# Groups of half a sequence, a ramp of 7, 9, 17, and one queue for the first loads, in a fused convolution and feed-forward kernel

## The chip, the cores and the metric

One core of one Trainium2 chip. The metric is the device time of one launch in microseconds (us); medians are over repeated launches. PE is the matmul engine (TensorE), PEld its weight load, DVE is VectorE, ACT is ScalarE, POOL is GpSimd; SP issues most transfers here. PSUM is the memory that PE writes its results into; this kernel takes eight buffers of 512 columns from it in a ring (`bufs=8`, tiles of `[P, 512]`), called banks here. "L264" in a profile line is a line of that kernel's source.

## The reference, cut to what matters

x is 8 sequences of 4224 tokens of 192 values. A causal convolution with 7 taps (one set of softmax weights for each of 8 heads), then layer normalisation, a feed-forward of 192 to 768 with relu and back to 192, and a residual sum:

```python
out = np.einsum('hk,bskhg->bshg', w, x_unf)          # 7 taps, 8 heads of 24 values
xn  = (x - mu) / np.sqrt(var + 1e-06) * g_ln
ch  = np.maximum(xn @ w_ch1, 0.0) @ w_ch2            # 192 -> 768 -> 192
return (x + ch).astype(np.float32)
```

w_ch1 and w_ch2 arrive as 64-bit floats and are rebuilt as 32-bit on the chip.

## The kernel before: the parts that matter

A partition holds 33 consecutive tokens ("runs") of a sequence. A group is some of these runs, for all 128 partitions. The small groups of the first sequence are called the ramp, since with them the pipeline fills; a seam is the change from one PE piece (an up or a down projection) to the next, and the tail is what follows the last matmul. For each group, VectorE convolves, transposes and takes statistics; PE does the up projection (tile `ph`), ScalarE the relu, PE the down projection (`po`), VectorE the scaled residual sum, which also empties `po`.

```python
J = 11
for b in range(B):
    sizes = [J] * (R // J) + [R % J] * (R % J > 0)   # 11, 11, 11
    if b == 0:
        rest = R - 15
        sizes = [7, 8, rest // 2, rest - rest // 2]  # 7, 8, 9, 9
...
nc.gpsimd.dma_start(out=ga, in_=g_col[0:P, :])       # gains: q0 software_dynamic in the profile
nc.sync.dma_start(out=taps, ...)
nc.scalar.dma_start(out=raw1[:, 1:3] ...)            # w1 on two queues, beside x
...
def up(g):                                           # 6 f-blocks
    for f in range(NF):
        ph = [psum.tile([P, 512], F32, tag="ps", ...) for q in range(NQ)]   # 4 of 8 banks
        for c in range(NC):
            for q in range(NQ):
                nc.tensor.matmul(ph[q][:, 0 : n * C], w1[rows, c, fs], t[rows, 0:n, c, :], ...)
        for q in range(NQ):
            nc.scalar.activation(ht[g][:, f, 0:n, q, :], ph[q]..., AF.Relu)

def down(g):
    for i0 in range(0, n, 2):                        # one bank for two runs
        po = psum.tile([P, 512], F32, tag="ps", ...)
        ...                                          # 6 matmuls a run
        nc.vector.scalar_tensor_tensor(out=yg[:, j, :], in0=dst, ...)       # empties it

first_tap(0); conv(0); centre_w1(); first_tap(1); transpose(0)
...                                                  # rebuild w2
for g in range(NG):
    if g + 2 < NG: load_x(g + 2)
    if g == 0: conv(1)
    up(g)
    if g + 1 < NG:
        if g > 0: first_tap(g + 1); conv(g + 1)
        transpose(g + 1)
    stats(g)
    down(g)
```

On VectorE the order within one pass of the loop is thus: convolve and transpose the next group, statistics of this group, then empty this group's `po`.

## Time and profile before

| | before |
|---|---|
| time, first three launches | 1081.26, 1082.58, 1081.49 us |
| span of the profiled execution | 1080.5 us |
| PE / DVE / ACT busy | 98% / 76% / 22% |

The profiled execution took 1082.24 us, so it is a little slower than the median launch. The engine table and the chain that ended last are in the prediction, with their lines.

### The profile page before, as it was taken

The numbers are of one execution on the slowest core, as the hardware profiler recorded it, in microseconds if no ns is written. First come the engines' busy times: TensorE is split into PE (matmuls) and PEld (weight loads), VectorE is DVE, ScalarE is ACT, GpSimd is POOL, SyncE is SP. The second block draws the span as 40 slices with busy tenths as digits, with TensorE's granted clock in tenths as the row PEclk, the third lists the DMA queues.
The fourth block names the chain that finished last, engine by engine and source line by source line (L and its number), as shares of the span: only waits on it lengthen the run. The fifth ranks groups of instructions, "written<-read, shape, count | busy, mean of one in ns | idle before, by whom it ended". The sixth has DMA issues, their size and how long they took to land.

```text
span 1080.5 us, 24335 instructions
## 1 busy us (share of the span) xinstructions
PE 1057.4 (98%) x10512; PEld 898.8 (83%) x10512; DVE 822.2 (76%) x2363; ACT 240.3 (22%) x636; POOL 16.9 (2%) x23
## 2 busy tenths in 40 slices
PE   3999999999999999999999999999999999999998
PEld 3999987978978879789788797897887978978878
DVE  5999798696696876966968769669687696696821
ACT  3521122031131220311312203113122031131220
POOL 3000000000000000000000000000000000000000
PEclk9999999999999999999999999999999999999999
DMA  8022022022022020230220302203202022020011
GB/s 241 2 82 89 4 96 96 30 75 103 2 103 89 16 104 31 74 103 1 104 102 3 103 31 74 104 1 103 102 2 103 32 73 104 1 104 41 2 42 41
DMA packets 9195, 70.55 MB, mean 65 GB/s; under 512 B 1280, under 2 KB 2304, under 8 KB 3329
## 3 DMA queue, kind: packets, MB, share of 16 engines
q1 hardware_dynamic: 8768, 68.02, 18.3%
q8 instruction: 82, 1.34, 0.5%
q10 hardware_dynamic: 224, 0.98, 0.4%
q14 instruction: 25, 0.20, 0.1%
q0 software_dynamic: 96, 0.00, 0.0%
HBM read 43.05 MB, written 25.95 MB: 64 GB/s over the span
## 4 chain that ended last, share of the span: by engine, by line
PE 96%; DVE 2%; DMA 1%; issue 0%; ACT 0%; ACTq 0%; DVEq 0%
PE po L352 48%; PE ph L329 48%; DVE y L265 1%; DMA raw<-in_moe_w_ch_dram 1%; DVE yt L273 0%; DVE w1f L184 0%; DVE scale1a L174 0%; ACT scale1b L166 0%; DVE scale1b L174 0%; DVE power1a L163 0%; DVE mant1a L157 0%; DVE power1a L159 0%; DVE y L357 0%; ACTq L130 0%; DVE power1b L163 0%
## 5 line engine op out<-in xcount | busy, mean ns | idle before, releaser
L352 PEld LDWEIGHTS po<-w,ht 128*128 128x128 f32 x3168 | 513.5, 190 | 13.3 <-issue 11.7
L352 PE MATMUL po<-w,ht 128*128 128x192 f32 x3168 | 522.5, 327 | 0.0
L329 PE MATMUL ph<-yt,w 32*128 32x352 f32 (+3 forms) x7200 | 520.4, 444 | 1.0 <-DVE yt L273 1.0
L329 PEld LDWEIGHTS ph<-yt,w 32*128 32x128 f32 x7200 | 367.4, 185 | 146.1 <-issue 5.4
L265 DVE SCALAR_TENSOR_TENSOR y<-xg,taps,y 128x264 f32<-128x264 f32 (+3 forms) x1200 | 473.7, 474 | 0.0
L334 ACT ACTIVATE ht<-ph 128x352 f32<-128x352 f32 (+3 forms) x600 | 222.7, 459 | 792.3 <-PE ph L329 792.3
L357 DVE SCALAR_TENSOR_TENSOR y<-po,r,y 128x192 f32<-128x192 f32 x264 | 96.5, 412 | 228.0 <-PE po L352 225.3
L286 DVE BATCH_NORM_STATS2 st<-y 128x6 f32<-128x192 f32 x264 | 70.1, 341 | 0.0
L273 DVE STREAM_TRANSPOSE yt<-y 128x2112 f32<-128x2112 f32 (+3 forms) x25 | 57.3, 2290 | 0.9
L257 DVE TENSOR_SCALAR y<-xg,taps 128x264 f32<-128x264 f32 (+1 forms) x184 | 51.4, 351 | 0.0
L237 PE MATMUL pw<-w1f,centre 128*128 128x128 f32 x144 | 18.0, 292 | 18.7 <-DVE w1f L184 18.7
L237 PEld LDWEIGHTS pw<-w1f,centre 128*128 128x128 f32 x144 | 17.9, 208 | 18.6 <-issue 18.6
L101 POOL MEMSET xg<- 1x1152 f32 x8 | 8.4, 1048 | 779.6 <-DVE y L265 779.6
L312 DVE SCALAR_TENSOR_TENSOR r<-d,r 128x11 f32<-128x11 f32 (+3 forms) x75 | 12.7, 170 | 2.6
L308 DVE TENSOR_TENSOR d<-r 128x11 f32<-128x11 f32 (+3 forms) x75 | 12.7, 170 | 2.6
L309 DVE SCALAR_TENSOR_TENSOR d<-d,v 128x11 f32<-128x11 f32 (+3 forms) x75 | 12.7, 170 | 2.6
L240 ACT COPY w<-pw 128x512 f32<-128x512 f32 (+1 forms) x12 | 5.7, 477 | 8.8 <-PE pw L237 8.6
L255 ACT ACTIVATE y<-xg,taps 128x168 f32<-128x168 f32 (+1 forms) x16 | 5.6, 432 | 0.0
L157 DVE TENSOR_SCALAR mant1a<-raw 128x768 uint32<-128x768 uint32 x1 | 0.6, 559 | 6.0 <-DMA raw<-in_moe_w_ch_dram 6.0
L289 DVE TENSOR_TENSOR d<-st 128x11 f32<-128x11 f32 (+3 forms) x25 | 4.4, 177 | 0.9
L300 DVE TENSOR_SCALAR d<-v 128x11 uint32<-128x11 uint32 (+3 forms) x25 | 4.3, 173 | 0.9
L297 DVE TENSOR_SCALAR v<-v 128x11 f32<-128x11 f32 (+3 forms) x25 | 4.3, 173 | 0.9
(46 smaller groups left out, 47.4 us busy)
## 6 DMA issues: line engine op xcount, KB each, us to landing
xg<-in_x_dram SPq DMA_DIRECT2D x14, 1632.0 KB, 9.2
out_dram<-y SPq DMA_DIRECT2D x20, 1056.0 KB, 4.9
xg<-in_x_dram SPq DMA_DIRECT2D x7, 1428.0 KB, 10.8
xg<-in_x_dram SPq DMA_DIRECT2D x2, 1440.0 KB, 12.5
out_dram<-y SPq DMA_DIRECT2D x2, 864.0 KB, 4.4
xg<-in_x_dram SPq DMA_DIRECT2D x1, 1344.0 KB, 14.1
xg<-in_x_dram SPq DMA_DIRECT2D x7, 191.2 KB
raw<-in_moe_w_ch_dram SPq DMA_DIRECT2D x1, 1152.0 KB
```

What stands on the lines that cost most here:

```text
L237: nc.tensor.matmul(dst, m[:, c, :], w1f[:, s, o : o + P], start=start, stop=not start)
L257: nc.vector.tensor_scalar(out=dst, in0=src, scalar1=tap, scalar2=None, op0=ALU.mult)
L265: nc.vector.scalar_tensor_tensor(out=y[g][:, 0:n, cs], in0=t[:, k : k + n, cs], scalar=taps[:, h, k : k + 1], in1=y[g][:, 0:n, cs], op0=AL ...
L273: nc.vector.transpose(yt[g][:, 0:n].rearrange("p j c t -> p (j c t)"), y[g][:, 0:n].rearrange("p j d -> p (j d)"),)
L286: nc.vector.bn_stats(out=st[:, j, :], in_=y[g][:, j, :])
L308: nc.vector.tensor_tensor(d, r, r, op=ALU.mult)
L309: nc.vector.scalar_tensor_tensor(out=d, in0=d, scalar=-0.5, in1=v, op0=ALU.mult, op1=ALU.mult)
L312: nc.vector.scalar_tensor_tensor(out=r, in0=d, scalar=1.5, in1=r, op0=ALU.add, op1=ALU.mult)
L329: nc.tensor.matmul(ph[q][:, 0 : n * C], w1[rows, c, fs], t[rows, 0:n, c, :], start=(c == 0), stop=(c == NC - 1),)
L334: nc.scalar.activation(ht[g][:, f, 0:n, q, :], ph[q][:, 0 : n * C].rearrange("p (j t) -> p j t", t=C), AF.Relu,)
L352: nc.tensor.matmul(dst, t[:, f, j, :, :].rearrange("p q t -> p (q t)"), w2[:, f, :], start=(f == 0), stop=(f == NF - 1),)
L357: nc.vector.scalar_tensor_tensor(out=yg[:, j, :], in0=dst, scalar=rstd[g][:, j : j + 1], in1=yg[:, j, :], op0=ALU.mult, op1=ALU.add,)
```

## The change

Its intent: fewer and larger groups, so fewer seams and fewer fixed costs on VectorE, and an earlier start, since w1 no longer shares the DMA engines with x (before, from 6 to 8 us, the queue that brings most of w1 took 60.1% of the 16 engines' time and SP's, with x and the rest of w1, 42.8%). Groups are 16 and 17 runs (the first sequence 7, 9, 17). 17 runs are 544 columns and do not fit the 512 of one bank, so they are halved to 9 and 8. Buffers of the setup are laid into the space of the first hidden tile to make room, and x has two buffers instead of three.

```diff
-    J = 11
+    J = 17
...
-        sizes = [J] * (R // J) + [R % J] * (R % J > 0)
-        if b == 0:
-            rest = R - 15
-            sizes = [7, 8, rest // 2, rest - rest // 2]
         j0 = 0
-        for n in sizes:
+        for n in (7, 9, R - 16) if b == 0 else (J - 1, J):
...
-    xpool = ctx.enter_context(tc.tile_pool(name="xin", bufs=3))
+    xpool = ctx.enter_context(tc.tile_pool(name="xin", bufs=2))
...
-    raw1 = setup.tile([P, 3, FH, 2], U32, name="raw1")
+    room = hpool.tile([P, NF * J * P], F32, tag="ht", name="room")
+    raw1 = carve(6 * FH, U32).rearrange("p (s f w) -> p s f w", f=FH, w=2)
...
-    nc.gpsimd.dma_start(out=ga, in_=g_col[0:P, :])
+    nc.scalar.dma_start(out=ga, in_=g_col[0:P, :])
...
-    nc.scalar.dma_start(
+    nc.sync.dma_start(
         out=raw1[:, 1:3].rearrange("p s f w -> p (s f w)"), in_=w1_words[0:P, :]
...
-        (nc.sync, nc.scalar)[r].dma_start(
+        nc.sync.dma_start(
...
+        half = n if n * C <= 512 else (n + 1) // 2
         for f in range(NF):
-            ph = [psum.tile([P, 512], F32, tag="ps", name=f"ph{g}_{f}_{q}") for q in range(NQ)]
+            for i0 in range(0, n, half):
+                js = slice(i0, min(i0 + half, n))
```

The small operations on the taps also move ahead of the rebuilding of w1, the rebuilding works in place, and the last group's stores end at 4, 8, 12, 14, 16, 17 runs.

More of the change, by code (lines that the diff above doesn't have):

```diff
@@ L56 @@
     FH = F // 2
-    assert D == P + Q and S % P == 0 and J * C <= 512 and NF % 2 == 0
+    assert D == P + Q and S % P == 0 and R % 2 and R // 2 + 1 == J and NF % 2 == 0
     groups = []
     for b in range(B):
-        sizes = [J] * (R // J) + [R % J] * (R % J > 0)
-        if b == 0:
-            rest = R - 15
-            sizes = [7, 8, rest // 2, rest - rest // 2]
         j0 = 0
-        for n in sizes:
+        for n in (7, 9, R - 16) if b == 0 else (J - 1, J):
             groups.append((b, j0, n))
             j0 += n
-        assert j0 == R and max(sizes) <= J
+        assert j0 == R
+    assert max(n for _, _, n in groups) <= J
     NG = len(groups)
@@ L117, with carve @@
     gb = consts.tile([P, 1], F32, name="gb")
-    raw1 = setup.tile([P, 3, FH, 2], U32, name="raw1")
+    room = hpool.tile([P, NF * J * P], F32, tag="ht", name="room")
+    taken = [0]
+    def carve(n, dtype):
+        part = room[:, taken[0] : taken[0] + n].bitcast(dtype)
+        taken[0] += n
+        return part
+    raw1 = carve(6 * FH, U32).rearrange("p (s f w) -> p s f w", f=FH, w=2)
     raw2 = setup.tile([P, NF * D, 2], U32, name="raw2")
@@ L122 @@
     g_col = moe_g_ln.rearrange("(d o) -> d o", o=1)
-    nc.gpsimd.dma_start(out=ga, in_=g_col[0:P, :])
+    nc.scalar.dma_start(out=ga, in_=g_col[0:P, :])
     for r in range(2):
-        nc.gpsimd.dma_start(out=gb[Q * r : Q * r + Q, :], in_=g_col[P:D, :])
+        nc.scalar.dma_start(out=gb[Q * r : Q * r + Q, :], in_=g_col[P:D, :])
     nc.sync.dma_start(
@@ L148, with split_words @@
     nc.vector.memset(low, -896.0 * (1 << 23))
-    def split_words(raw, name):
-        n = raw.shape[1]
+    def split_words(raw, mant, power):
         hi = raw[:, :, 1]
-        mant = setup.tile([P, n], I32, name="mant" + name)
-        power = setup.tile([P, n], I32, name="power" + name)
-        high = setup.tile([P, n], F32, name="high" + name)
-        scale = setup.tile([P, n], I32, name="scale" + name)
         nc.vector.tensor_single_scalar(mant.bitcast(U32), hi, 0xFFFFF, op=ALU.bitwise_and)
-        nc.scalar.activation(high, mant, AF.Relu, scale=2.0**-20, bias=1.0)
+        nc.scalar.activation(mant.bitcast(F32), mant, AF.Relu, scale=2.0**-20, bias=1.0)
         nc.vector.tensor_scalar(
@@ L165, in split_words, with join_words @@
         )
-        nc.scalar.activation(scale, power, AF.Relu, scale=float(1 << 23), bias=low)
-        return high, scale
-    def join_words(dst, raw, high, scale, gain=None):
+        nc.scalar.activation(power, power, AF.Relu, scale=float(1 << 23), bias=low)
+    def join_words(dst, raw, mant, power, gain=None):
         lo, hi = raw[:, :, 0], raw[:, :, 1]
+        mant, power = mant.bitcast(F32), power.bitcast(U32)
         nc.vector.scalar_tensor_tensor(
-            out=high, in0=lo, scalar=2.0**-52, in1=high, op0=ALU.mult, op1=ALU.add
+            out=mant, in0=lo, scalar=2.0**-52, in1=mant, op0=ALU.mult, op1=ALU.add
         )
         nc.vector.scalar_tensor_tensor(
-            out=scale.bitcast(U32), in0=hi, scalar=0x80000000, in1=scale.bitcast(U32),
+            out=power, in0=hi, scalar=0x80000000, in1=power,
             op0=ALU.bitwise_and, op1=ALU.bitwise_or,
         )
+        power = power.bitcast(F32)
         if gain is None:
-            nc.vector.tensor_tensor(dst, high, scale.bitcast(F32), op=ALU.mult)
+            nc.vector.tensor_tensor(dst, mant, power, op=ALU.mult)
             return
@@ L184, in join_words @@
             nc.vector.scalar_tensor_tensor(
-                out=dst[:, part], in0=high[:, part], scalar=g, in1=scale.bitcast(F32)[:, part],
+                out=dst[:, part], in0=mant[:, part], scalar=g, in1=power[:, part],
                 op0=ALU.mult, op1=ALU.mult,
             )
-    w1f = setup.tile([P, 3, FH], F32, name="w1f")
+    w1f = carve(3 * FH, F32).rearrange("p (s f) -> p s f", f=FH)
     raw1a = raw1[:, 0:2].rearrange("p s f w -> p (s f) w")
@@ L199 @@
     nc.scalar.activation(taps, taps, AF.Exp)
-    parts_a = split_words(raw1a, "1a")
     nc.vector.tensor_reduce(wsum, taps, axis=AX.X, op=ALU.add)
@@ L206 @@
     )
-    join_words(w1f[:, 0:2].rearrange("p s f -> p (s f)"), raw1a, *parts_a, (gb, ga))
-    parts_b = split_words(raw1b, "1b")
-    join_words(w1f[:, 2], raw1b, *parts_b, (ga,))
+    words_a = (raw1a, carve(2 * FH, I32), carve(2 * FH, I32))
+    words_b = (raw1b, carve(FH, I32), carve(FH, I32))
+    split_words(*words_a)
+    join_words(w1f[:, 0:2].rearrange("p s f -> p (s f)"), *words_a, (gb, ga))
+    split_words(*words_b)
+    join_words(w1f[:, 2], *words_b, (ga,))
     w1 = consts.tile([P, NC, F], F32, name="w1")
@@ L218 @@
     for i, (p0, p1, base) in enumerate(((0, P, 0), (0, Q, P), (Q, P, P))):
-        m = setup.tile([P, NC, NQ, C], F32, name=f"centre{i}")
+        m = carve(NC * P, F32).rearrange("p (c q i) -> p c q i", c=NC, q=NQ)
         if p1 - p0 < P:
@@ L322, in up @@
         ht[g] = hpool.tile([P, NF, J, NQ, C], F32, tag="ht", name=f"ht{g}")
+        half = n if n * C <= 512 else (n + 1) // 2
         for f in range(NF):
             fs = slice(f * P, f * P + P)
-            ph = [psum.tile([P, 512], F32, tag="ps", name=f"ph{g}_{f}_{q}") for q in range(NQ)]
-            for c in range(NC):
+            for i0 in range(0, n, half):
+                js = slice(i0, min(i0 + half, n))
+                w = (js.stop - js.start) * C
+                ph = [
+                    psum.tile([P, 512], F32, tag="ps", name=f"ph{g}_{f}_{i0}_{q}")
+                    for q in range(NQ)
+                ]
+                for c in range(NC):
+                    for q in range(NQ):
+                        rows = slice(C * q, C * q + C)
+                        nc.tensor.matmul(
+                            ph[q][:, 0:w], w1[rows, c, fs], t[rows, js, c, :],
+                            start=(c == 0), stop=(c == NC - 1),
+                        )
                 for q in range(NQ):
-                    rows = slice(C * q, C * q + C)
-                    nc.tensor.matmul(
-                        ph[q][:, 0 : n * C], w1[rows, c, fs], t[rows, 0:n, c, :],
-                        start=(c == 0), stop=(c == NC - 1),
-                    )
-            for q in range(NQ):
-                nc.scalar.activation(
-                    ht[g][:, f, 0:n, q, :],
-                    ph[q][:, 0 : n * C].rearrange("p (j t) -> p j t", t=C), AF.Relu,
-                )
+                    nc.scalar.activation(
+                        ht[g][:, f, js, q, :],
+                        ph[q][:, 0:w].rearrange("p (j t) -> p j t", t=C), AF.Relu,
+                    )
     def down(g):
@@ L342, in down @@
         yg = y.pop(g)
-        ends = (n,) if g + 1 < NG else (4, 8, 10, n)
+        ends = (n,) if g + 1 < NG else (4, 8, 12, 14, 16, n)
         done = 0
@@ L374 @@
     transpose(0)
-    parts = split_words(raw2, "2")
-    join_words(w2flat, raw2, *parts)
+    words_2 = (
+        raw2, setup.tile([P, NF * D], I32, name="mant"), setup.tile([P, NF * D], I32, name="power")
+    )
+    split_words(*words_2)
+    join_words(w2flat, *words_2)
     for g in range(NG):
```

## The prediction

> **What bounds the kernel now.** I read the page's engine table first, then the chain that ended last, then the groups by shape, then the timeline where groups meet.
>
> ```profile
> PE 1057.4 (98%) x10512; PEld 898.8 (83%) x10512; DVE 822.2 (76%) x2363; ACT 240.3 (22%) x636; POOL 16.9 (2%) x23
> ```
>
> TensorE is busy 98% of the 1080.5 us span, and VectorE has a quarter of its time free. Saving VectorE instructions is worth nothing by itself. The chain says which PE pieces there are and what comes ahead of them (start, length, what):
>
> ```profile
> 1.20 11.83 DMA raw<-in_moe_w_ch_dram
> ...
> 21.27 14.70 DVE y L265 x48
> ...
> 37.71 14.71 PE ph L329 x283
> 52.43 13.85 PE po L352 x84
> 66.27 16.88 PE ph L329 x288
> 83.15 15.80 PE po L352 x96
> 98.95 17.67 PE ph L329 x288
> 116.62 17.75 PE po L352 x108
> ...
> 1033.92 21.51 PE ph L329 x288
> 1055.44 21.71 PE po L352 x132
> ```
>
> The time is thus three terms: 37.7 us before the first up projection (load w1, rebuild it, convolve group 0, transpose), then 1039.4 us in which up (ph) and down (po) pieces follow without a gap, then a tail of 3.3 us. A change can only shorten the prologue, the cost of a seam between pieces, or the tail; and it can open a gap.
>
> The seams: a group of 9 runs costs 17.67 and one of 11 21.51 in ph. The timeline shows relu evictions of successive f-blocks at steps of 2.27, 2.59, 2.91 and 3.55 us for 7, 8, 9 and 11 runs: 0.03 + 0.32 x runs. Six steps leave 0.21 us per up piece. The down piece is 0.20 + 1.95 x runs (evictions of two runs every 3.90 us), plus 0.05 at 11 runs, a wait for ScalarE.
>
> ```profile
> 66.20 16.95 PE L329 MATMUL ph<-yt,w 32*128 32x256 f32 x288
> ...
> 67.52 2.37 DVE L357 SCALAR_TENSOR_TENSOR y<-po,r,y 128x192 f32<-128x192 f32 x7
> 69.15 1.22 ACT L334 ACTIVATE ht<-ph 128x256 f32<-128x256 f32 x4 [15.94 <-PE ph L329]
> 69.61 13.14 PEld L329 LDWEIGHTS ph<-yt,w 32*128 32x128 f32 x236 [0.36 <-DVE y L357]
> ...
> 72.42 1.21 ACT L334 ACTIVATE ht<-ph 128x256 f32<-128x256 f32 x4 [2.05 <-PE ph L329]
> 75.01 1.21 ACT L334 ACTIVATE ht<-ph 128x256 f32<-128x256 f32 x4 [1.38 <-PE ph L329]
> ```
>
> This is the one existing stall after the prologue. The second f-block of group 1 (8 runs) needs the PSUM buffers of group 0's down piece; VectorE, in program order behind convolution, transpose and statistics, empties them only from 67.52 to 69.89. The block was due at 66.20 + 2.59 = 68.8, so 1.1 us are lost: 16.88 against 6 x 2.59 + 0.21 = 15.75. PSUM buffers go round in a ring of 8, and a late VectorE stops PE through it.
>
> [...]306, 331, 356 and 406 ns pitch (busy over count) for 7, 8, 9 and 11 runs is 131 + 25 x runs. [...]768 KB of w1 on ACT's queue took 8.7 us to land beside x.
>
> **The change, part by part.**
>
> *Steady state.* 25 groups become 17, but the halving makes the 17-run groups two blocks, 9 and 8 wide: still 25 blocks and 7200 up matmuls, and 3168 down. One batch before: 3 x (21.51 + 21.70) = 129.63. After: up(16) = 6 x (0.03 + 5.12) + 0.21 = 31.11; up(17) = 6 x (2.91 + 2.59) + 0.21 = 33.21; down(17) = 0.20 + 33.15 = 33.35. For down(16), the first run's sixth matmul pair needs all four relu evictions of the last f-block.
>
> ```profile
> 536.97 1.53 ACT L334 ACTIVATE ht<-ph 128x352 f32<-128x352 f32 x4 [2.02 <-PE ph L329]
> ...
> L352 PE MATMUL po<-w,ht x25: 326/326/430, 536.9 to 540.9; 128*128 128x192 f32 x25
> ```
>
> The four take 1.53 us at 352 columns, and a matmul of that stretch waits up to 0.1 us (430 against 326 ns). At 224 columns they take 1.11, so 0.82 ns a column each; at 512, 2.05. The wait grows by 0.52 to 0.57: down(16) = 0.20 + 31.20 + 0.57 = 31.97. Batch after: 31.11 + 31.97 + 33.21 + 33.35 = 129.64. The seams saved are given back to ScalarE: **0.0 us** in seven batches. VectorE saves 8 x 48 x 131 ns = 50 us, all off the path. In steady state it reaches the evictions about 40 us into a 17-run group (taps 2.8, convolution of 16 runs 25.5, transpose 3.4, statistics 7.7), 6.6 us after down starts: 3.4 runs, two banks, so no stall.
>
> *Prologue.* The windows show what the first loads share:
>
> ```profile
> 6.00:8.00 2.00, 0.00 (x0) 0.00 (x0) 0.43 (x2) 0.25 (x1) 1.89 (x3) 1.00 1.04 198
> ...
> 20.00:22.00 2.00, 2.00 (x12) 2.00 (x11) 1.83 (x5) 2.00 (x8) 0.00 (x0) 1.00 1.01 430
> ```
>
> (last column GB/s). w1 is 1.18 MB and was complete at 13.0. Alone in order it starts when the 128 small packets of taps are through (5.3 in the packet list) and needs 2.7 us at 430 GB/s or 5.4 at 220, then about 1 us to be seen: 9.1 to 11.7. I take 10.3, so 2.9 us earlier. The four small tap operations (14.70 to 15.52) now run before w1 lands; the join still waits for ScalarE, so I count 0.6. x for group 0 follows in the queue at about 11 to 16 and is wanted by ScalarE some 6.3 us after w1, 16.6: hidden. Centring on PE, 18.0 us from 15.2, ends at 33.2, before the transpose. The rest (convolution of 7 runs, 14.7; transpose, 1.6) is as before: up(0) starts at **34.2, gain 3.5 us**.
>
> *Ramp 7, 9, 17.* Counted from the start of up(0). VectorE before: evictions of group 0 from 29.8 to 32.2. Convolving 9 runs instead of 8 adds 48 x 25 ns = 1.2, transpose 0.2: 31.2 to 33.6. up(1) starts at 28.5, and its second block is due at 31.4: stall 33.6 - 31.4 = 2.2. down(1) ends at 28.5 + 17.67 + 2.2 + 17.75 = 66.1. VectorE meanwhile: first tap of 17 runs (8 x 360 ns = 2.9) to 36.4, convolution 48 x (131 + 425) = 26.7 to 63.0, transpose (178 + 200 x 17 = 3.6) to 66.6, statistics of 9 (5.55) to 72.1, first pair of evictions to 72.8. up(2) needs the transpose at 66.6, and then four PSUM buffers. down(1) holds five of eight, so the fourth comes free only at 72.8. PE **stalls 6.7 us**. In the kernel before, the group there had 9 runs and its evictions began at 96.06, ahead of PE at 98.9: no stall. Stalls go from 1.1 to 8.9: +7.8. The first batch has one group less: 0.4 saved. Convolving 16 runs during group 2 catches up, so the stall is paid once.
>
> *Tail.* Last store one run of 96 KB in both: 0.
>
> Sum: 1081.5 - 3.5 + 7.8 - 0.4 + 0.0 = **1085.4 us**.
>
> **The rivals.** (1) The seams are really won: no ScalarE wait at 512 columns, 7 x 0.57 = 4.0 us less, 1081.4. For it: [...]only 0.1 us is seen now. Against: the eviction time per column is a clean line. (2) The ramp stall does not come, if something empties down(1) sooner: 1085.4 - 7.8 = 1077.6. For it: someone chose 9 and 17 on purpose. Against: VectorE keeps program order in every stretch of the timeline, and the 1.1 us stall shows the mechanism. (3) The early w1 is no gain, because the slow stretch from 6 to 17 us has another cause than sharing (it still moves 203 to 257 GB/s after ACT's queue is done): up to 1088; or the full 430 GB/s: 1084. (4) Two x buffers instead of three expose a load. A 17-run load is 23 x 96 KB = 2.2 MB, some 13 us scaled from 9.2 us for 1632 KB, issued about 65 us ahead: hidden. If not, each group could lose microseconds, 1100 and more; I give it little.
>
> **Range and chances.** Terms (1) and (3) can each move the sum by 3 to 4 us, the stall by 1.5: 1081 to 1089 holds it 8 times in 10. 2% is 21.6 us, far outside all but rival (4). Faster 0.01, within 2% 0.98, slower 0.01.
>
> **What would show it.** In the changed profile: first up matmul at about 34; w1 complete near 10; a gap or lengthened ph piece of 6 to 7 us about 66 us after that, with the PE load waiting for the VectorE eviction of group 1; from then up pieces of 31.1 and 33.2 and down pieces of 32.0 and 33.4; a wait of 0.6 us at each 16-run seam; VectorE busy near 770. A first up start above 36, no stall at group 2, or down(16) of 31.4 would each mark its step wrong; waits for x in mid kernel would make the whole prediction wrong.

The marked cuts take out what no trace of this case shows. The sum came to 1081.5 - 3.5 + 7.8 - 0.4 + 0.0 = 1085.4 us. Its 0.03 + 0.32 x runs and 131 + 25 x runs are fits to the steps and pitches read from the trace; what the 0.03 is made of was not shown. The "about 1 us to be seen" is read from the kernel before: from the end of a load's last packet to the moment it counts as landed the trace has 1.1 us for the taps (5.5 to 6.6) and 1.0 and 1.6 for w1's loads on ScalarE's queue.

## The result, and the profile after

The changed kernel takes 1089.37 us (median of 6, 1088.55 to 1089.68), the kernel before 1081.34 (6 launches). The ratio is 1.0072, 95% interval 1.0059 to 1.0085. Ratios here are the mean time of one kernel's fast runs over that of the other's in the same rounds, so not quite the ratio of the medians quoted. The measured time lies just above the stated range.

The engine table of the changed kernel:

```profile
PE 1060.4 (97%) x10512; PEld 905.1 (83%) x10512; DVE 744.6 (68%) x1779; ACT 240.3 (22%) x636; POOL 15.2 (1%) x20
```

As many matmuls as before, 3 us more PE time, 78 us less VectorE time. The chain of the changed kernel (start, length, what):

```profile
2.25 7.71 DMA room<-in_moe_w_ch_dram
...
15.02 19.24 PE pw L241 x144
...
98.42 3.58 DVE yt L277
...
107.52 0.75 DVE y L369 x2
108.32 35.71 PE ph L341 x549
144.03 33.35 PE po L364 x204
177.38 31.15 PE ph L341 x288
208.53 2.05 ACT ht L346 x4
210.62 29.84 PE po L364 x182
240.47 33.21 PE ph L341 x576
```

Before, the chain was PE without a break from 37.7 us on. Now it runs through VectorE up to 108.3 us: that is the ramp in which PE waits. w1 is complete at 10 us instead of 13. From 144 us on it is again PE, with one 2.05 us piece of ScalarE in each 16-run group. And one piece stands out: the same 17-run up projection takes 35.71 us at 108.32 and 33.21 us later. The timeline where it starts:

```profile
83.82 17.82 PE L364 MATMUL po<-w,ht 128*128 128x192 f32 x108
102.15 0.76 PE L341 MATMUL ph<-yt,w 32*128 32x288 f32 x6 [0.51 <-DVE yt L277]
107.52 3.02 DVE L369 SCALAR_TENSOR_TENSOR y<-po,r,y 128x192 f32<-128x192 f32 x9
108.32 21.88 PE L341 MATMUL ph<-yt,w 32*128 32x288 f32 x332 [5.41 <-DVE y L369]
```

The down projection of group 1 ends at 101.6. Six matmuls of group 2 go out when its transpose is done; the next needs a PSUM bank that VectorE starts to empty at 107.52. From 101.6 to 108.3, 6.7 us, PE does next to nothing. What follows is in the window table (stretch and its length, then busy time of PE, PEld, DVE, ACT and POOL with the number of instructions that fall into the stretch, then the granted PE clock, the DMA share and GB/s):

```profile
102.00:106.00 4.00, 0.76 (x6) 0.34 (x6) 3.74 (x19) 0.00 (x0) 0.00 (x0) 1.00 0.00 0
107.00:108.00 1.00, 0.00 (x0) 0.00 (x0) 0.82 (x4) 0.00 (x0) 0.00 (x0) 0.50 0.00 0
108.50:113.00 4.50, 4.50 (x40) 3.35 (x44) 4.50 (x15) 0.00 (x0) 0.00 (x0) 0.50 0.39 141
114.00:119.00 5.00, 5.00 (x92) 4.48 (x88) 5.00 (x11) 2.10 (x7) 0.00 (x0) 1.00 1.01 419
```

While PE waits, its granted clock falls to 0.50 (at 106.48 us in the trace's clock record), and it stays there until 113.30, for the first five microseconds after the wait: 40 matmuls in 4.5 us where 92 fit into 5 us later. "PE busy" reads 4.50 of 4.50 in the slow stretch; only the clock and the count tell.

### The profile page after: what moved, and what is told of

Same layout as the page of the kernel before. It is cut to its first block, busy times and chain, and to the rows that moved or that the text cites. A ratio compares the mean times of both kernels' runs of the same rounds, so it can differ in the third digit from the quotient of the medians.

```text
span 1087.9 us, 23679 instructions
## 1 busy us (share of the span) xinstructions
PE 1060.4 (97%) x10512; PEld 905.1 (83%) x10512; DVE 744.6 (68%) x1779; ACT 240.3 (22%) x636; POOL 15.2 (1%) x20
## 4 chain that ended last, share of the span: by engine, by line
PE 90%; DVE 7%; ACT 2%; DMA 1%; issue 0%; SPq 0%; DVEq 0%
PE ph L341 45%; PE po L364 44%; DVE y L269 4%; PE pw L241 2%; ACT ht L346 1%; DMA room<-in_moe_w_ch_dram 1%; DVE yt L277 1%; DVE st L290 0%; DVE y L369 0%; DVE y L261 0%; DVE mant L172 0%; DVE w L181 0%; DVE power L175 0%; DVE room L186 0%; DVE d L312 0%
## 5 line engine op out<-in xcount | busy, mean ns | idle before, releaser
L341 PE MATMUL ph<-yt,w 32*128 32x288 f32 (+3 forms) x7200 | 522.2, 445 | 7.3 <-DVE y L369 5.7
L269 DVE SCALAR_TENSOR_TENSOR y<-xg,taps,y 128x408 f32<-128x408 f32 (+3 forms) x816 | 423.6, 603 | 0.0
L346 ACT ACTIVATE ht<-ph 128x288 f32<-128x288 f32 (+3 forms) x600 | 222.6, 457 | 790.5 <-PE ph L341 790.5
L277 DVE STREAM_TRANSPOSE yt<-y 128x3264 f32<-128x3264 f32 (+3 forms) x17 | 55.8, 3284 | 0.6
L261 DVE TENSOR_SCALAR y<-xg,taps 128x408 f32<-128x408 f32 (+1 forms) x120 | 41.8, 422 | 0.0
L241 PE MATMUL pw<-room 128*128 128x128 f32 x144 | 19.2, 304 | 15.0 <-DVE room L186 15.0
L241 PEld LDWEIGHTS pw<-room 128*128 128x128 f32 x144 | 19.1, 220 | 15.0 <-issue 15.0
L312 DVE TENSOR_TENSOR d<-r 128x17 f32<-128x17 f32 (+3 forms) x51 | 9.0, 176 | 1.8
L313 DVE SCALAR_TENSOR_TENSOR d<-d,v 128x17 f32<-128x17 f32 (+3 forms) x51 | 9.0, 176 | 1.8
L316 DVE SCALAR_TENSOR_TENSOR r<-d,r 128x17 f32<-128x17 f32 (+3 forms) x51 | 8.9, 175 | 1.8
```

The lines of the kernel that those rows point to most:

```text
L241: nc.tensor.matmul(dst, m[:, c, :], w1f[:, s, o : o + P], start=start, stop=not start)
L261: nc.vector.tensor_scalar(out=dst, in0=src, scalar1=tap, scalar2=None, op0=ALU.mult)
L269: nc.vector.scalar_tensor_tensor(out=y[g][:, 0:n, cs], in0=t[:, k : k + n, cs], scalar=taps[:, h, k : k + 1], in1=y[g][:, 0:n, cs], op0=AL ...
L277: nc.vector.transpose(yt[g][:, 0:n].rearrange("p j c t -> p (j c t)"), y[g][:, 0:n].rearrange("p j d -> p (j d)"),)
L312: nc.vector.tensor_tensor(d, r, r, op=ALU.mult)
L313: nc.vector.scalar_tensor_tensor(out=d, in0=d, scalar=-0.5, in1=v, op0=ALU.mult, op1=ALU.mult)
```

## The experiments

My theory after reading this: the ramp costs what the prediction said, the 6.7 us wait, and **the wait also costs the clock**. The rivals: the large groups themselves cost in the steady state; the single queue costs; the slow matmuls after the wait have another reason than the clock. Each kernel ran five rounds beside the kernel before on the same chip, so ratios, not medians, are what compares across sections.

### ramp_7_8_8_10: the ramp alone

```diff
-        for n in (7, 9, R - 16) if b == 0 else (J - 1, J):
+        for n in (7, 8, 8, 10) if b == 0 else (J - 1, J):
```

> The changed kernel with the first sequence as 7, 8, 8, 10 in place of 7, 9, 17; all else as changed. Theory (a late VectorE holds the PSUM buffers of group 1, PE idles 6.7 us before group 2 and then runs at half clock): the stall and the half clock after it go, PE pieces of the first sequence end near 167.5 us instead of 177.4, so about 1079.5 us, 10 us under the changed kernel. Rival one, the cost is in the large groups of the steady state (wait for the 512-wide evictions): stays within 1 us of 1089. Rival two, the cost is in the single load queue: also stays near 1089.

Measured: 1078.88 us, ratio 0.9978 (0.9965 to 0.9990). Its chain has no VectorE piece in the ramp, and the seven later sequences start at 166.17 instead of 177.38:

```profile
126.88 19.59 PE ph L341 x288
146.47 19.70 PE po L364 x120
166.17 31.15 PE ph L341 x288
```

The steady state is untouched here and the time falls by some 10 us, as the theory has it. Both rivals that leave the loss outside the ramp are out. How far a group may grow can be estimated from the durations in the prediction: with n runs in PE's hands and m runs next, VectorE needs about 11.0 + 1.5 m + 0.3 n us (tap, convolution and transpose of m, statistics of n, first eviction) and PE gives it 0.4 + 3.9 n. For m = 17 and n = 9 that is 39.2 us; the changed kernel's VectorE took 39.2 (69.03 to 108.28). So m may be at most about 2.4 n - 7: 8 after 7, 10 after 8, 16 after 10, but not 17 after 9. The estimate takes it that VectorE starts on the next group when PE starts on this one; before group 2 of the changed kernel it started 5.1 us after PE, which made the stall longer.

### ramp_7_8_9_9: a smaller stall, on purpose

```diff
-        for n in (7, 9, R - 16) if b == 0 else (J - 1, J):
+        for n in (7, 8, 9, 9) if b == 0 else (J - 1, J):
```

> The changed kernel with the first sequence as it was before the change, 7, 8, 9, 9. Theory: the same balance that sets the stall before group 2 of the changed kernel now says that a group of 9 followed by one of 16 stalls PE by 2.9 us (first eviction pair of the 9-run group done about 2.9 us after PE needs its buffer)[...]: about 1082.3 us, up to 1084 if it drops. Rivals one and two: stays near 1089.

Measured: 1082.92 us (median of 5, 1080.62 to 1083.19), ratio 1.0011. The estimate above lets 14 follow 9, and here 16 does: a stall came where it said. The down projection before it ends at 166.85 and PE goes on at 169.65, 2.8 us later, as expected. Line of the timeline and of the window table at that place:

```profile
169.65 8.85 PE L341 MATMUL ph<-yt,w 32*128 32x512 f32 x64 [1.73 <-DVE y L369]
```

```profile
170.50:173.80 3.30, 3.30 (x20) 1.39 (x20) 3.30 (x11) 0.00 (x0) 0.00 (x0) 0.53 0.35 145
```

I had expected that so short a stall (the weight load is idle 2.56 us, the matmuls 1.73) would probably leave the clock alone, an estimate that no run had shown (cut from the expectation, where "if it drops" means the clock). In the profiled run it did not: the clock record has 0.50 from 170.16 to 173.58. The five timed runs split: 1083.19, 1083.18 and 1082.92 us have a mean clock of 0.998, 1080.62 and 1082.42 one of 1.000. So whether a stall of this length costs the clock differs between executions of the same program.

### keep_warm: the wait stays, the idleness goes

```diff
+                if (g, f, i0) == (2, 0, 0):
+                    for _ in range(18):
+                        nc.tensor.matmul(
+                            ph[0][:, 0:D], w1[:, 0, 0:P], w2[:, 0, :], start=True, stop=True
+                        )
```

> The changed kernel with 18 idle matmuls (5.85 us of PE) put before the first up block of group 2, into a buffer that the real matmuls overwrite; no wait is taken away. Theory (idle PE loses its clock): the wait for VectorE stays, the up matmuls of group 2 then run at full pace from the start, 33.2 us in place of 35.7: 2.4 us less, 1087.0. Rival, the slow matmuls after the wait come from VectorE reading the same PSUM or from the order of the buffers: no change, 1089.4, or a little more.

Measured: 1086.32 us, ratio 1.0048 (1.0034 to 1.0062), mean clock 1.000. Useless work made the kernel faster. The timeline has the idle matmuls and the eviction that PE still waits for; in the chain, group 2's up projection is the last of these lines:

```profile
100.16 6.01 PE L340 MATMUL ph<-w,w 128*128 128x192 f32 x36
106.21 3.02 DVE L374 SCALAR_TENSOR_TENSOR y<-po,r,y 128x192 f32<-128x192 f32 x9
```

```profile
107.00 33.26 PE ph L346 x549
```

33.26 us against 35.71, as expected: VectorE still empties the banks at the same point of its order, and PSUM is read while PE writes just as before, so the slow stretch came from the clock and from nothing else at that place. The start moved too, from 108.32 to 107.00, which this edit cannot do; see warm_start. So of the 3 us between the medians some 2.5 belong to the edit, and the rest to the start.

### loads_alone: the other half of the change

The groups of before (7, 8, 9, 9, then 11), three x buffers, and the new loads and setup.

```diff
-    J = 17
+    J = 11
-        for n in (7, 9, R - 16) if b == 0 else (J - 1, J):
+        for n in (7, 8, 9, 9) if b == 0 else (J, J, J):
-    xpool = ctx.enter_context(tc.tile_pool(name="xin", bufs=2))
+    xpool = ctx.enter_context(tc.tile_pool(name="xin", bufs=3))
-        ends = (n,) if g + 1 < NG else (4, 8, 12, 14, 16, n)
+        ends = (n,) if g + 1 < NG else (4, 8, 10, n)
```

> The groups of before (7, 8, 9, 9, then 11; three x buffers) with the one queue, the new order of loads and the setup in place of the changed kernel. Theory: only the prologue's gain is left; group 1 starts its up projection at 63.9 in place of 66.2 us, so 2.3 us under before, 1079.0. Rival two (the single queue costs): above before, 1083 or more. Rival one: as the theory.

Measured: 1078.94 us, ratio 0.9979 (0.9967 to 0.9992). The loads and setup gain 2.2 us. It equals ramp_7_8_8_10 (0.9978), which has large groups: so the larger groups are worth nothing in the steady state, as the prediction's 0.0 said. The profiles agree: the seven later sequences take 907.3 us here and 907.55 there.

### old_queues: the loads undone

```diff
-    nc.scalar.dma_start(out=ga, in_=g_col[0:P, :])
+    nc.gpsimd.dma_start(out=ga, in_=g_col[0:P, :])
...
-    nc.sync.dma_start(out=raw1[:, 1:3] ...)
+    nc.scalar.dma_start(out=raw1[:, 1:3] ...)
-        nc.sync.dma_start(out=raw1[Q * r ...)
+        (nc.sync, nc.scalar)[r].dma_start(out=raw1[Q * r ...)
```

> The changed kernel with the first loads put back on the queues of before (gains on the software queue, w1 split over two hardware queues beside x). Theory: w1 is seen near 13 us instead of 10, and everything after it moves by as much: 3 us more, about 1092.4, give or take 1 us for the moment at which the PE clock rises. Rival (the earlier w1 is worth nothing, some other term set the prologue): no change, 1089.4.

Measured: 1091.12 us, ratio 1.0088 (4 fast runs, 1.0074 to 1.0102), that is 1.7 us above the changed kernel by the ratios, not 3. The first operation on w1 starts at 11.65 us here, 10.10 in the changed kernel and 13.16 in the kernel before, which has the same queues. So about half of w1's earlier arrival comes with the queues. What the other 1.5 us are was not settled.

### halve_16 and ramp_and_halve: the wait for wide evictions

```diff
-        half = n if n * C <= 512 else (n + 1) // 2
+        half = n if n * C < 512 else (n + 1) // 2
```

> The changed kernel with groups of 16 runs also halved (8 and 8), so no up block is 512 columns wide. Theory: the wait of 0.57 us at each 16-run seam goes, each of the seven up pieces takes 0.18 us more (twelve blocks of 2.59 instead of six of 5.15), net 0.39 us seven times: 2.7 us less, about 1086.7. Rival one of the prediction (the wide evictions are the main cost of the large groups) would want 5 us or more; if the wait is an artefact of the record and costs nothing, the time rises by 1.3 us to 1090.6.

Measured: 1087.54 us, ratio 1.0052 (1.0039 to 1.0064). The chain of this kernel:

```profile
305.05 17.03 PE ph L341 x309
322.95 14.94 PE ph L341 x267
...
435.85 31.29 PE ph L341 x576
467.14 31.40 PE po L364 x192
```

Where nothing disturbs it, a 16-run group takes 31.29 + 31.40 = 62.69 us, against 240.47 - 177.38 = 63.09 in the changed kernel: the wait was real, and 0.40 us is won, as worked out. But the second such group has a gap at 322 us that the profile puts down to no engine ("issue", 0.86 us) and takes 1.6 us longer in all, and two others are 0.1 and 0.4 us longer. These take back 2.1 of the 2.8 us; the seven sequences take 906.87 us against 907.55. So only 0.7 us of the difference of some 2 us between the ratios is the halving's; the rest lies before the seven sequences, where this edit changes nothing, and is the spread of the start and of the clock that the last experiments show. An instruction packet of 1.7 us ended just ahead of the gap in the packet list. The same group loses 2.0 us in ramp_and_halve and 1.5 in early_tap, each time within 0.5 us of the end of an instruction packet of 1.5 to 1.9 us, where most take about 1.0; that it is the cause is not shown.

With the repaired ramp as well:

> Both repairs: first sequence 7, 8, 8, 10 and groups of 16 halved. If the two are independent: 1078.9 less 2.7, about 1076.2, below the kernel before and the changed one.

Measured: 1077.02 us, ratio 0.9957 (0.9943 to 0.9970). The time is near the expected one, but for another reason in part: by the profiles the seven later sequences take 0.3 us less than in ramp_7_8_8_10 (907.26 against 907.55), not 2.7, and they start 0.7 us earlier after a shorter centring (17.8 us against 18.2).

### early_tap: the best version tried

```diff
     conv(0)
-    centre_w1()
     first_tap(1)
+    centre_w1()
     transpose(0)
```

on top of ramp_and_halve.

> As both repairs, and ScalarE computes the first tap of group 1 ahead of the copies of the centred w1 instead of after them. In the changed kernel the w2 rebuild waits for ScalarE (2.7 us) behind those copies and that tap, and group 0's evictions wait behind the rebuild (1.1 us of PE). Theory: both waits go, convolution of group 1 starts near 40 us instead of 42.6, up of group 1 near 62 instead of 63.9: about 2.6 us less than both repairs, 1073.6. Rival (the first tap then waits for x and holds up the copies, so that PE runs out of PSUM buffers in the centring): no gain or a loss.

Measured: 1076.32 us, ratio 0.9952 (0.9939 to 0.9964), the fastest of all, 0.5% below the kernel before. Against ramp_and_halve the intervals overlap, and the expected 2.6 us did not come: I had taken the waits of the changed kernel's profile, but in the profile of ramp_and_halve the centring happened to be faster (see next) and up of group 1 started at 61.9 us anyway, 61.2 with the early tap.

### after_again, warm_start, warm_both: what the clock costs in all

Besides the stall, one more term of the prediction was off: the up projection of group 1 started at 63.9 us, not at 62.7. The centring of w1 on PE took 19.24 us (18.02 before), because 28 of its 144 passes were spaced at 0.213 us and the others at 0.112; in the kernel before only 16 were slow. (The expectation below says 17; the count is 16.) ScalarE copies its results, and the first tap of group 1 and the w2 rebuild wait behind those copies. First the centring of the kernel before (timeline) and a stretch of it, then two stretches of the changed kernel's:

```profile
18.66 18.02 PE L237 MATMUL pw<-w1f,centre 128*128 128x128 f32 x144 [18.66 <-DVE w1f L184]
20.70:22.70 2.00, 2.00 (x14) 2.00 (x13) 1.97 (x6) 2.00 (x8) 0.00 (x0) 1.00 1.02 432
19.00:21.00 2.00, 2.00 (x11) 2.00 (x11) 2.00 (x8) 0.90 (x3) 0.00 (x0) 1.00 0.57 242
21.00:23.00 2.00, 2.00 (x19) 2.00 (x19) 2.00 (x8) 0.32 (x1) 0.00 (x0) 1.00 0.01 4
```

The clock column is no help here: it reads 1.00 where the trace has no clock record yet. The record begins with the full clock at 22.25 us in the kernel before and at 21.14 in the changed one, 3.6 and 6.1 us after the first pass, and in both the spacing of the passes shortens at that moment.

```diff
+    spin = consts.tile([P, P], F32, name="spin")
+    nc.vector.memset(spin, 0.5)
...
+                if (f, c0) == (0, 0):
+                    for _ in range(50):
+                        nc.tensor.matmul(pw[:, 0:P], spin, spin, start=True, stop=True)
```

> The changed kernel unaltered, on the chip of the next two for a direct comparison: about 1089.4.

> The changed kernel with 50 idle 128x128 matmuls on PE from about 1 us, before the centring matmuls that wait for w1 at 15 us. Theory: in the changed kernel the first 28 passes of the centring ran at half clock (17 in the kernel before), so ScalarE's copies and the first tap and w2 rebuild behind them came late, and 1.2 us of the prologue's gain were lost there. Started warm, centring takes 16.1 us (144 passes of 0.112) in place of 19.2, and up of group 1 starts near 62.3 us in place of 63.9: about 1.6 us less, 1087.8. Rival (the late tap has another cause, such as x landing late): no change.

> Both idle fillings, at the start and before group 2: the wait for VectorE stays as it is, only the half clock is gone. Theory: 1089.4 - 2.5 - 1.6 = 1085.3, which is where the prediction stood, because the prediction had everything but the clock.

Measured on one chip: after_again 1088.84 us (1087.34 to 1089.90), ratio 1.0071; warm_start 1087.22, ratio 1.0055; warm_both 1084.65 (1084.23 to 1084.94), ratio 1.0032. warm_both's centring takes 16.32 us, the clock of its profiled run is 1.000 (two of its five timed runs show 0.998), and its group 2 is (chain, then window table):

```profile
105.33 33.26 PE ph L351 x549
```

```profile
105.50:110.00 4.50, 4.50 (x80) 4.10 (x84) 4.50 (x15) 1.32 (x4) 0.00 (x0) 1.00 0.40 136
```

80 matmuls in 4.5 us where the changed kernel did 40. After_again's own profile shows the spread of the unfilled start: there the centring took 17.86 us, up of group 1 started at 62.4 and the span was 1085.6, 2.3 less than in the first profile of the same program. With both fillings the spread is smaller: 0.7 us over the five runs of warm_both, 2.6 over those of after_again. Without the half clock the changed kernel is 3.2 us slower than before (by the medians), but the kernel before keeps its own slow start there, so this is not like with like; keep_warm is the fairer check (next section).

What a stall of the same kind costs in clock differs too. Five profiles wait for group 2 with nothing filled in; up of group 2 is 33.26 us where the wait is filled:

| | up of group 2 | more than 33.26 | from restart to full clock |
|---|---|---|---|
| after | 35.71 | 2.45 | 4.98 |
| after_again | 34.97 | 1.71 | 3.49 |
| old_queues | 35.72 | 2.46 | 5.00 |
| halve_16 | 35.15 | 1.89 | 3.85 |
| warm_start | 36.20 | 2.94 | 5.98 |

All in us; the wait is 6.7 us in each. The loss is about half of the time from the restart to the full clock. In the clock records the half clock lasts 6.83 us in four of them, 10.24 in warm_start and 3.41 in ramp_7_8_9_9: two, three and one times 3.41 (the mean clocks of those profiled runs, 0.997, 0.995 and 0.998, agree).

## Why the prediction was wrong

Predicted 1085.4, range 1081 to 1089; measured 1089.37. Step by step, by the profiles:

| Step of the prediction | predicted | measured |
|---|---|---|
| first operation on w1 | 10.3 | 10.10 |
| up(0) starts | 34.2 | 34.2 |
| up(1) starts | 34.2 + 28.5 = 62.7 | 63.9 |
| up(1) with its stall | 17.67 + 2.2 | 19.88 |
| PE waits before group 2 | 6.7 | 101.6 to 108.3: 6.7 |
| **up(2)** | **33.21** | **35.71** |
| down(17); up(16) | 33.35; 31.11 | 33.35; 31.15 |
| down(16) with its wait | 31.97 | 31.94 |
| seven sequences | 907.5 | 907.55 |
| tail | 3.3 | 3.0 |
| VectorE busy | near 770 | 744.6 |

**The mechanism of the wait, and every wait, were right.** The ring of eight banks, VectorE's order, the 6.7 us stall, the seam that ScalarE takes back and the zero in the steady state all came as worked out; ramp_7_8_8_10 and loads_alone show that this stall is what turns the change from a gain of 0.2% into a loss.

**The step that failed** is "PE stalls 6.7 us", with "the stall is paid once": it priced the stall as the idle time alone. It was paid once, but for 6.7 + 2.5 us, since PE came out of it at half clock. keep_warm shows it: the wait left in place and the idleness filled, the 2.5 us are gone. That is the term of the sum that was mis-sized: 7.8 should have been 10.3. The 2.5 is one sample; the table above has 1.7 to 2.9.

**A second term** is in the prologue. That the rest "is as before", with up(0) at 34.2, was right for the start but not for what hangs on it; and the start was right in part by luck: the prediction had the centring end at 33.2, a microsecond before the transpose, and it ended at 34.25, after it (33.92). "Centring on PE, 18.0 us" was a sample of a quantity that varies with the clock, 17.8 to 19.2 us in the profiles here. At 19.24 it made ScalarE late and up(1) 1.2 us later, so that of the prologue's 3.5 us only 2.3 remained. warm_start and after_again support it: with 16.3 us of centring up(1) starts at 61.7, and in the unaltered kernel with 17.86 at 62.4, beside the predicted 62.7.

The span grew by 1087.9 - 1080.5 = 7.4 us against 3.9 forecast, 3.5 more. The two terms are 3.7 of it, and the tail gave 0.3 back. The medians are 4.0 us from the forecast, 0.5 more: the forecast added its terms to 1081.5, but read them from an execution of 1082.24. keep_warm, which takes away the half clock of the stall alone, had a centring near the predicted one (18.25 us), and its profile is the predicted one: up(1) at 62.6, up(2) from 107.0 for 33.26, span 1084.1 against 1080.5 + 3.9 = 1084.4. warm_both ends at 1084.65, 0.75 below the predicted 1085.4; by its span (1082.5) it is 1.9 below, mostly because its filled start makes the centring 1.7 us shorter than the 18.0 that the prediction had. That it comes near the predicted time is thus partly chance.

**What I could have seen.** The profile of the kernel before already has PE work at a slower pace: the first 16 of the centring's 144 passes came at 0.213 us, those after 22.25 us, where the clock record begins, at 0.112. I worked out a PE stall of 6.7 us and did not ask what the clock does. The prediction's range allowed the stall an error of 1.5 us, and this was 2.5.

**The rivals.** (1), seams really won: the wait for wide evictions is real, 0.40 us each net (halve_16), and was already in the sum. (2), no ramp stall: refuted. (3), the early w1 is no gain: refuted by loads_alone, 2.2 us for loads and setup together, of which old_queues puts 1.7 down to the queues. Its premise held, though: in one queue the core still moved 143 to 264 GB/s from 6 to 14 us, and 415 to 453 from 16 to 20; what sets the slow stretch was not shown. (4), two x buffers: no wait for x shows in mid kernel. VectorE's busy time was mis-sized because I left out the 16 small statistics operations and the first-tap overheads of eight groups; off the path, it cost nothing. (The pitches of 306 to 406 ns in the prediction are those of VectorE's convolution operations.)

## What to carry to other kernels

When one engine feeds another through a ring of buffers, check the ramp separately from the steady state: the next group's preparation must fit into the current group's matmul time, so group sizes may only grow by a bounded factor (here about 2.4 n - 7, an estimate). Price a PE stall as its length plus the half clock that can follow it (here 1.7 to 2.9 us after some 6.7), and look at the granted clock and the count of matmuls, since busy time hides it. A change made of two parts with opposite signs should be run as its two parts.
